# The second batch's q by a casting DMA, and loads in another order, in a fused attention and SwiGLU kernel

## The chip, the cores and the metric

The kernel runs on one core of a Trainium2 chip. The metric is the device time of one execution in microseconds. The kernel before took 332.03 us (median of 3 runs, 331.59 to 332.16). TensorE is the matrix engine (PE in the profile, its weight loads PEld), VectorE is DVE, ScalarE is ACT, GpSimd is POOL, and SyncE (SP) only issues transfers.

## The reference

There are 8 batches of 8 heads with 576 positions and a head width of 64. A linear attention without softmax is normalized per head, its rows become 4608 tokens of width 512, and these go through an RMS norm and a SwiGLU block of inner width 1536:

```python
kv = np.einsum('bhsd,bhse->bhde', k, v)
out = np.einsum('bhsd,bhde->bhse', q, kv)
rms = np.sqrt(np.mean(out * out, axis=-1, keepdims=True) + 1e-06)
x = (out / rms * g_norm)                      # per head, then heads side by side: [4608, 512]
rms = np.sqrt(np.mean(x * x, axis=-1, keepdims=True) + 1e-06)
xn = x / rms * rms_g
g = xn @ w_gate
out = (g * (1.0 / (1.0 + np.exp(-g))) * (xn @ w_val)) @ w_out
```

Inputs and output are float32; the kernel computes its matrix products in bf16 with float32 sums.

## The kernel before

**Tiles.** A batch's 576 positions are four chunks of 128 and a remainder of 64. The remainders of the 8 batches are collected in `xr`, 512 tokens that form a ninth group at the end. So there are nine groups of 512 tokens, each with the same SwiGLU work: for each of 12 column blocks of 128 a gate product (`mm1` with `wg`, L618), its Silu on ScalarE (L627), a value product (`mm1` with `wv`), and the product of the two on VectorE (`h`, L636); then `mm2` (L653) with `wo`, whose results are copied out (L669) and stored by SP (L671). `mm1` rotates over three PSUM buffers: a gate's buffer is freed by its Silu, a value's by its `h`.

**Attention of a batch** goes on beside the SwiGLU of the batch before. q is loaded and made bf16, and is needed transposed (`qTs`). `kv_mm` (L267) forms k'v head by head, with results 64 wide in alternating halves of the partitions; `kv_half` copies the two halves (L291) to `kvs`. `o_mm` (L318) multiplies. The squares of the result are reduced per head, a chain of small VectorE steps turns them into one factor `al` per token and head that holds both norms, and `xna_` (L465) applies it; a transpose then gives `x`.

- The first batch (L774 to L873) is done by hand with transposes on TensorE, spread through the first half of its own SwiGLU. That group is split into two halves of 256 tokens: 22 "early" slots for the first, 12 "half" slots (a gate and a value each) for the second, then 16 "all" slots that run `mm2` block by block (`slots_b_by_j`), three matmuls in each.
- The second batch is placed by hand in `place_second(P, 9)`: numbers are slots relative to the tenth half slot. Its q comes by SP in float32 (`load_q(1)`, released by the last gate weights), is cast by VectorE and ScalarE (L202), and transposed on TensorE by pairs of heads (L297, 128 x 128 each). Its statistics come from a matmul with `sel` (L390) and its factor from the 12-step chain with a bit-trick root (`chain`). The first batch's first half uses a shorter form, `lead_chain` with Sqrt on ScalarE, which needs a `guard` matmul that adds the epsilon (L373).
- Batches 3 to 8 come from `place_attention`, where a `Placer` puts each operation into the first slot with room on its engine. q is loaded by SP in float32 (L180), cast by ScalarE (third batch) or GpSimd (the others), and transposed by a DMA on SP (L311, L313). VectorE reduces the squares (L401), GpSimd weighs them with the gain first (L396).

**Loads.** v, k (from the second batch on) and all weights come by casting DMAs on GpSimd's queue (`load_cast`, `load_w`, `load_wo`), issued in the order of the code: weights, v and k of the second batch, the four pieces of `wo`, k and v of the third batch. There are eight semaphores for these transfers, so each issue waits until the transfer eight places ahead of it has landed. Engines run their instructions in order, so an instruction that waits holds all behind it. Within a slot the operations of other engines are emitted ahead of the slot's own matmuls, those of TensorE behind them. The place of later loads is set at the end of the code (L909 to L920): `P.put` from a given slot on.

Of the kernel before, what the change touches and what calls it, by code (L numbers as in the profile page):

```python
# [86 lines left out]
def kernel(  # L87
# [53 lines left out]
    vc, kc = ([consts.tile([128, H, (NC + 1) * D], BF16, name=f"{t}c{n}") for n in range(2)] for t in "vk")  # L141
    sel = consts.tile([128, 2, 2], BF16, name="sel")
    diag = consts.tile([128, 2 * D], BF16, name="diag")
    ones = consts.tile([1, 128], FP32, name="ones")
    epsr = consts.tile([1, 2 * H], FP32, name="epsr")
    gain = consts.tile([128, NS], FP32, name="gain")
# [37 lines left out]
    def load_cast(b, t, heads=None):  # L184
        to = (vc if t == 2 else kc)[b % 2]
        if heads is None:
            return nc.gpsimd.dma_start(  # L187
                out=to[:REM, :, NC * D :], in_=src[t][b, :, MAIN:S, :].rearrange("h p d -> p h d")
            )
        view = src[t][b, :, 0:MAIN, :].rearrange("h (p c) d -> p h (c d)", c=NC)[:, heads[0] : heads[1]]  # L190
        return nc.gpsimd.dma_start(out=to[:, heads[0] : heads[1], : NC * D], in_=view)  # L191
# [44 lines left out]
    class Att:  # L236
# [56 lines left out]
        def qT_mm(self, js, chunks, pool=None):  # L293
# [7 lines left out]
            return qT_ps  # L301

        def qT_out(self, ps, js, c0, eng):
            copy = eng.copy if eng is nc.scalar else eng.tensor_copy
            n = ps.shape[2] // 128
            to = self.qTj[:, js[0] : js[-1] + 1, c0 : c0 + n, :]
            copy(out=to, in_=ps.rearrange("p j (c t) -> p j c t", t=128))
# [77 lines left out]

        def stat_mm(self, c0, c1):
            self.st = st = att_p.tile([128, 2, NC + 1, H], FP32, name="att")
            for c in range(c0, c1):
                for j in range(NS):
                    nc.tensor.matmul(  # L390
                        st[:, :, c, 2 * j : 2 * j + 2], lhsT=self.sqT[:, j, c], rhs=sel,
                        start=c == c0 and j == 0, stop=c == c1 - 1 and j == NS - 1, skip_group_check=True,
                    )
# [130 lines left out]
    def place_casts(P, b, at=0):  # L524
# [5 lines left out]
        ops = [P.put("POOL", 1.1, lambda hs=hs: cast_main(b, 0, nc.gpsimd, hs), at=at) for hs in (H0, H1)]  # L530
        return [P.put("POOL", 0.65, lambda: cast_rem(b, 0, nc.gpsimd), at=max(at + 9, ops[1][1]))]

# [27 lines left out]
    def place_second(P, s):  # L560
# [7 lines left out]

        dve(-1, 0.7, lambda: cast_main(1, 0, V, H0))
        act(-1, 1.04, lambda: cast_main(1, 0, A, H1))  # L570
        for j in range(NS):
            pe(j // 2, 0.23, ("q", j), lambda j=j: a.qT_mm((j,), range(NC)))
        P.at("PE", 1.14, lambda: a.kv_mm(range(NS)), s)
        dve(1, 0.42, lambda: a.qT_out(ps["q", 0], (0,), 0, V))
        act(1, 0.58, lambda: a.qT_out(ps["q", 1], (1,), 0, A))
        dve(1, 0.43, lambda: a.kv_half(0))
        dve(2, 0.43, lambda: a.kv_half(1))
        dve(2, 0.42, lambda: a.qT_out(ps["q", 2], (2,), 0, V))
        act(2, 0.58, lambda: a.qT_out(ps["q", 3], (3,), 0, A))
        act(2, 0.62, lambda: cast_rem(1, 0, A))  # L580
        pe(3, 0.23, ("q", NC), lambda: a.qT_mm(ALL, (NC,)))
        act(4, 0.58, lambda: a.qT_out(ps["q", NC], ALL, NC, A))

# [5 lines left out]
        for n in range(NC + 1):  # L589
            act((4, 5, 5, 6, 7)[n], 0.62, lambda n=n: a.sqT_(ps["oT", n], *parts[n]))  # L590
            dve((4, 5, 6, 6, 7)[n], 0.69, lambda n=n: a.outa_(n, V))
        P.at("PE", 0.64, lambda: a.stat_mm(0, NC + 1), s + 8)
        dve(9, 2.8, lambda: [f() for f in a.chain(0, NC + 1)])
        for c in range(NC + 1):
# [169 lines left out]
    G.memset(kvs[1], 0.0)  # L764
    for tile_ in (kc[0], kc[1], vc[1]):
        G.memset(tile_[REM:, :, NC * D :], 0.0)
# [44 lines left out]

    for j, pool_, eng in zip(ALL, (o2_p, o2_p, None, mm1_p), (A, A, V, V)):
        a.xT_mm((j,), (0, 1), pool_)
        a.xT_out(j, (0, 1), eng)
# [3 lines left out]
    cast_rem(0, 0, G)  # L818
    for t in (2, 1):
        load_cast(1, t, (0, H))  # L820
        load_cast(1, t)
# [13 lines left out]
    def behind(n):  # L835
# [27 lines left out]
        elif n == 18:  # L863
            a.xna_pairs(held[2], ALL, NC, NC + 1)
        if n in (15, 18):
            i = (15, 18).index(n)
            a.xT_mm((P0, P1)[i], (2, 3), None if i else o2_p)
# [7 lines left out]
    for n, s in enumerate(early):  # L875
        if n == 12:
            gate = load_q(1)
            tc.add_manual_dep(gate.ins, w_loads[-1][0].ins.name, SYNC, reason="the weights come first")
            nc.sync.dma_start(out=gbc, in_=g_norm.partition_broadcast(128))
        emit([s])  # L880
# [5 lines left out]
    gate = load_q(2)  # L886
    tc.add_manual_dep(gate.ins, wo_loads[1].ins.name, SYNC, reason="the weights come first")

# [10 lines left out]
    for b in range(1, B):  # L899
# [16 lines left out]
        elif b + 1 < B:  # L916
            P.put("SP", 0.0, lambda b=b: load_q(b + 1), at=starts[b - 1] + 6 * (b == 2))
            for f in loads_kv(b + 1):
                P.put("POOL", 0.85, f, at=starts[b - 1] + 6)
            casts = place_casts(P, b + 1, starts[b - 1] + 5 + 6 * (b == 2))  # L920
    emit(slots)
# [28 lines left out]
```

## Time and profile before

| | |
|---|---|
| median of 3 runs | 332.03 us |
| profiled execution | 331.74 us |
| its span in the trace | 330.0 us |
| TensorE busy | 318.1 us, 96% of the span |
| VectorE, ScalarE, GpSimd busy | 177.6, 143.1, 86.8 us |
| granted TensorE clock | 1.0 throughout |
| DMA | 41.08 MB, mean 124 GB/s |

Times in the profile are microseconds from the start of the span. A row of the timeline gives the start, the length, the engine, the line of the kernel, the operation, what it writes and reads, and how many instructions are merged; brackets at the end hold the idle time of that engine ahead of it and what ended it. Matmuls are pipelined, and their ends are modelled: successive rows overlap by the tail of the last matmul.

### The profile page before, as it was taken

What the parts mean: (1) busy time and instruction counts of PE and PEld (TensorE: products, weight loads), DVE (VectorE), ACT (ScalarE), POOL (GpSimd) and SP (SyncE); (2) the same over time, 40 slices, a digit from 0 to 9 for tenths busy, and PEclk for the clock granted to TensorE, in tenths of its full rate; (3) what the DMA queues carried; (4) which work ended last, traced back from release to release, by engine and by line L of the source; (5) the groups of instructions that cost most, each with busy time, mean ns of one, the idle gap of its engine ahead of it and who ended that gap; (6) DMA issues with size and microseconds to landing.
All of it is one profiled execution on the core that took longest, in us unless ns stands there. A gap on an engine that the chain in (4) does not pass through costs nothing.

```text
span 330.0 us, 5391 instructions
## 1 busy us (share of the span) xinstructions
PE 318.1 (96%) x2038; PEld 162.6 (49%) x2038; DVE 177.6 (54%) x400; ACT 143.1 (43%) x268; POOL 86.8 (26%) x106
## 2 busy tenths in 40 slices
PE   7899989989999999999999999999999999999995
PEld 2477865544445444544454445444544444444443
DVE  3448557667938780778167816872587234203411
ACT  1474463666548522742275217522752243223320
POOL 8653150026105700580049004900330000000000
PEclk9999999999999999999999999999999999999999
DMA  8999999995367966697869665986000600030014
GB/s 196 225 201 198 238 204 237 185 204 115 73 169 186 137 70 165 178 129 87 170 175 128 89 169 175 114 102 167 35 1 0 167 34 0 2 120 7 0 34 95
DMA packets 78741, 41.08 MB, mean 124 GB/s; under 512 B 42744, under 2 KB 74236, under 8 KB 78716
## 3 DMA queue, kind: packets, MB, share of 16 engines
q1 hardware_dynamic: 47616, 26.25, 34.9%
q0 software_dynamic: 29360, 13.57, 32.4%
q10 hardware_dynamic: 1740, 0.92, 1.0%
q8 instruction: 16, 0.26, 0.3%
q14 instruction: 9, 0.07, 0.1%
HBM read 37.78 MB, written 9.44 MB: 143 GB/s over the span
## 4 chain that ended last, share of the span: by engine, by line
PE 81%; DMA 15%; issue 1%; POOL 1%; DVE 0%; ACT 0%; SPq 0%; POOLq 0%; ACTq 0%
PE mm L618 47%; PE o L653 26%; DMA stg<-in_q_dram 7%; DMA wg<-in_moe_w_gate_dram 6%; DMA vc<-in_v_dram 3%; PE att L318 2%; PE att L267 2%; PE mm L653 2%; PE o L682 1%; POOL sq L396 0%; PE att L297 0%; PE att L355 0%; PE att L491 0%; ACT silu L627 0%; POOL vc L187 0%
## 5 line engine op out<-in xcount | busy, mean ns | idle before, releaser
L636 DVE TENSOR_TENSOR h<-silu,mm 128x512 bf16<-128x512 bf16 (+1 forms) x120 | 75.7, 631 | 80.6 <-PE mm L618 68.2
L627 ACT ACTIVATE silu<-mm 128x512 bf16<-128x512 f32 (+1 forms) x120 | 66.1, 555 | 89.2 <-PE mm L618 81.9
L618 PE MATMUL mm<-x,wv 128*128 128x512 bf16 (+1 forms) x432 | 99.8, 356 | 1.0 <-ACT silu L627 0.9
L618 PE MATMUL mm<-x,wg 128*128 128x512 bf16 (+1 forms) x420 | 98.5, 358 | 1.1 <-DVE h L636 1.1
L653 PE MATMUL o<-wo,h 128*128 128x512 bf16 x396 | 89.9, 379 | 0.0
L396 POOL TENSOR_TENSOR sq<-sq,g 128x512 bf16<-128x512 bf16 x30 | 34.4, 1154 | 131.1 <-ACT sq L344 131.0
L618 PEld LDWEIGHTS <-wg 128*128 128x128 bf16 x468 | 45.2, 98 | 46.8 <-issue 1.4
L618 PEld LDWEIGHTS <-wv 128*128 128x128 bf16 x480 | 45.3, 98 | 42.5 <-issue 1.1
L653 PEld LDWEIGHTS <-h 128*128 128x128 bf16 x420 | 40.4, 98 | 46.8
L669 ACT COPY osb<-o 128x512 f32<-128x512 f32 x33 | 19.3, 588 | 67.9 <-PE o L653 65.9
L401 DVE TENSOR_REDUCE st<-sq 128x8 f32<-128x512 bf16 x60 | 38.5, 679 | 2.1 <-POOL sq L396 2.1
L291 DVE CAST kvs<-att 64x256 bf16<-64x256 f32 x14 | 5.9, 422 | 39.4 <-PE att L267 39.2
L465 DVE TENSOR_TENSOR xna<-outa,al 128x512 bf16<-128x512 bf16 x35 | 21.8, 685 | 0.0
L344 ACT ACTIVATE sq<-att 128x512 bf16<-128x512 f32 x30 | 18.1, 603 | 0.8 <-PE att L318 0.8
L348 ACT CAST outa<-att 128x512 bf16<-128x512 f32 x30 | 17.7, 590 | 0.0
L318 PE MATMUL att<-kvs,qTs 128*128 128x128 bf16 x140 | 11.7, 219 | 1.5 <-DMA qTs<-main_q 1.5
L318 PEld LDWEIGHTS <-qTs 128*128 128x128 bf16 x140 | 9.7, 98 | 7.0 <-DMA qTs<-main_q 2.0
L618 PE MATMUL mm<-xr,wg 128*128 128x512 bf16 x48 | 12.3, 379 | 0.0
L618 PE MATMUL mm<-xr,wv 128*128 128x512 bf16 x48 | 12.3, 379 | 0.0
L202 POOL CAST main_q<-stg 128x1024 bf16<-128x1024 f32 (+1 forms) x12 | 11.4, 978 | 2.9 <-DMA stg<-in_q_dram 2.9
L231 PE MATMUL mm<-idle 128*128 128x512 bf16 x27 | 8.7, 484 | 2.1 <-DVE idle L160 2.1
L191 POOL DMA_DIRECT2D vc<-in_v_dram x9 | 7.9, 877 | 5.4 <-DMA kc<-in_k_dram 4.4
(118 smaller groups left out, 173.9 us busy)
## 6 DMA issues: line engine op xcount, KB each, us to landing
out_dram<-osb SPq DMA_DIRECT2D x32, 256.0 KB, 2.6
stg<-in_q_dram SPq DMA_DIRECT2D x7, 1024.0 KB, 6.9
vc<-in_v_dram POOLq DMA_DIRECT2D x7, 512.0 KB, 7.5
kc<-in_k_dram POOLq DMA_DIRECT2D x7, 512.0 KB, 6.1
wg<-in_moe_w_gate_dram POOLq DMA_DIRECT2D x4, 384.0 KB, 16.2
wv<-in_moe_w_val_dram POOLq DMA_DIRECT2D x4, 384.0 KB, 17.9
wo<-in_moe_w_out_dram POOLq DMA_DIRECT2D x4, 384.0 KB, 18.1
stg<-in_k_dram SPq DMA_DIRECT2D x2, 512.0 KB, 6.6
```

Source lines behind the costliest of these rows:

```text
L202: return copy(out=mains[b, t][:, cs[0] : cs[1], h0:h1, :], in_=staged[b, t].rearrange("p h (c d) -> p c h d", c=NC)[:, cs[0] : cs[1], h0:h ...
L318: nc.tensor.matmul(o[:, 2 * j : 2 * j + 2, :], lhsT=self.qTj[:, j, c, :], rhs=self.kv[:, j, :, :], start=j == 0, stop=j == NS - 1, skip_gr ...
L344: nc.scalar.activation(out=self.sq[c][:, 0], in_=self.o[c], func=ACT.Square)
L348: (eng.tensor_copy if eng else nc.scalar.copy)(out=self.outa[c], in_=self.o[c])
L396: eng.tensor_tensor(out=self.sq[c][:, 1], in0=self.sq[c][:, 0], in1=g2, op=OP.mult)
L401: nc.vector.reduce_sum(out=self.st[:, which, c, :], in_=self.sq[c][:, which], axis=AX.X)
L465: return eng.tensor_tensor(out=self.xna[:, c], in0=src, in1=self.al[:, c, :].to_broadcast([128, H, D]), op=OP.mult)
L618: nc.tensor.matmul(ps[:, : c1 - c0], lhsT=w[n][:, s, jj * 128 : (jj + 1) * 128], rhs=x_of(g, s, c0, c1), start=s == 0, stop=s == NS - 1)
L627: nc.scalar.activation(out=sis[g, j][:, c0:c1], in_=ps, func=ACT.Silu)
L636: nc.vector.tensor_tensor(out=hs[g, j][:, c0:c1], in0=sis[g, j][:, c0:c1], in1=v_ps, op=OP.mult)
L653: nc.tensor.matmul(ps, lhsT=hs[g, j][:, t * 128 : (t + 1) * 128], rhs=wo[j // OB][:, j % OB, :], start=j == 0, stop=j == NF - 1)
L669: (eng.copy if eng is nc.scalar else eng.tensor_copy)(out=o, in_=ps)
```

## The change

The change has these parts.

- The second batch's q comes by a casting DMA on GpSimd's queue into `qc`, ahead of v and k of that batch; `load_q(1)` and its three casts are gone. One more memset on GpSimd clears the remainder's rows of `qc`.
- It is transposed by heads (`qT_heads`): 40 matmuls with results 64 wide in alternating halves of the partitions, in five blocks of 8, in half slots 5 to 9 (counted from one), where 20 matmuls stood in slots 10, 11 and the first "all" slot. `kv_mm` moves from the tenth to the twelfth half slot, both its copies to the slot after it.
- The second batch's factor comes from `lead_chain` (four VectorE steps, Sqrt on ScalarE, one more step), with a guard matmul of 40 columns and two table loads on ScalarE, Sqrt ahead and Silu behind.
- The load of the third batch's q is released by the first piece of `wo` instead of the second.
- The fourth batch's k and v are placed from slot 14 of the second group's SwiGLU on instead of 6, and its q's casts from 18 instead of 11; for the later batches 14 instead of 6 and 18 instead of 5, and the remainder's cast directly behind the others. In GpSimd's program the casts of a batch's q now stand behind all five L396 of the batch before; of the fourth batch's k and v the main piece of k stands ahead of the fifth L396, the rest behind the casts.
- In the first batch, two of the transposes' copies swap between ScalarE and VectorE, and one transpose goes one slot later.

```diff
+    qc = consts.tile([128, H, (NC + 1) * D], BF16, name="qc1")
-    epsr = consts.tile([1, 2 * H], FP32, name="epsr")
+    epsr = consts.tile([1, (NC + 1) * H], FP32, name="epsr")
...
     def load_cast(b, t, heads=None):
-        to = (vc if t == 2 else kc)[b % 2]
+        to = qc if t == 0 else (vc if t == 2 else kc)[b % 2]
...
+        def qT_heads(self, js, chunks):
+            qT_ps = att_p.tile([128, len(js), len(chunks) * 128], BF16, name="att")
+            for n, j in enumerate(js):
+                for i, c in enumerate(chunks):
+                    for half in range(2):
+                        nc.tensor.matmul(
+                            qT_ps[half * D : (half + 1) * D, n, i * 128 : (i + 1) * 128],
+                            lhsT=qc[:, 2 * j + half, c * D : (c + 1) * D], rhs=ident, is_transpose=True,
+                            start=True, stop=True, skip_group_check=True,
+                        )
+            return qT_ps
...
-        def stat_mm(self, c0, c1):
+        def stat_mm(self, c0, c1, guard=False):
             self.st = st = att_p.tile([128, 2, NC + 1, H], FP32, name="att")
+            if guard:
+                nc.tensor.matmul(
+                    st[:, 0, c0:c1, :], lhsT=ones, rhs=epsr[:, : (c1 - c0) * H], start=True, stop=True, skip_group_check=True,
+                )
...
-        return [P.put("POOL", 0.65, lambda: cast_rem(b, 0, nc.gpsimd), at=max(at + 9, ops[1][1]))]
+        return [P.put("POOL", 0.65, lambda: cast_rem(b, 0, nc.gpsimd), at=ops[1][1])]
...
-        dve(-1, 0.7, lambda: cast_main(1, 0, V, H0))
-        act(-1, 1.04, lambda: cast_main(1, 0, A, H1))
         for j in range(NS):
-            pe(j // 2, 0.23, ("q", j), lambda j=j: a.qT_mm((j,), range(NC)))
-        P.at("PE", 1.14, lambda: a.kv_mm(range(NS)), s)
-        dve(1, 0.42, lambda: a.qT_out(ps["q", 0], (0,), 0, V))
-        act(1, 0.58, lambda: a.qT_out(ps["q", 1], (1,), 0, A))
-        dve(1, 0.43, lambda: a.kv_half(0))
-        dve(2, 0.43, lambda: a.kv_half(1))
-        dve(2, 0.42, lambda: a.qT_out(ps["q", 2], (2,), 0, V))
-        act(2, 0.58, lambda: a.qT_out(ps["q", 3], (3,), 0, A))
-        act(2, 0.62, lambda: cast_rem(1, 0, A))
-        pe(3, 0.23, ("q", NC), lambda: a.qT_mm(ALL, (NC,)))
-        act(4, 0.58, lambda: a.qT_out(ps["q", NC], ALL, NC, A))
+            pe(j - 5, 0.25, ("q", j), lambda j=j: a.qT_heads((j,), range(NC)))
+            if j % 2:
+                act(j - 4, 0.58, lambda j=j: a.qT_out(ps["q", j], (j,), 0, A))
+            else:
+                dve(j - 4, 0.42, lambda j=j: a.qT_out(ps["q", j], (j,), 0, V))
+        pe(-1, 0.25, ("q", NC), lambda: a.qT_heads(ALL, (NC,)))
+        act(0, 0.58, lambda: a.qT_out(ps["q", NC], ALL, NC, A))
+        P.at("PE", 1.14, lambda: a.kv_mm(range(NS)), s + 2)
+        dve(3, 0.43, lambda: a.kv_half(0))
+        dve(3, 0.43, lambda: a.kv_half(1))
...
-        P.at("PE", 0.64, lambda: a.stat_mm(0, NC + 1), s + 8)
-        dve(9, 2.8, lambda: [f() for f in a.chain(0, NC + 1)])
+        P.at("PE", 0.64, lambda: a.stat_mm(0, NC + 1, True), s + 8)
+        act(8, 1.28, lambda: A.preload_act_table(ACT.Sqrt))
+        dve(9, 2.0, lambda: a.lead_chain(0, NC + 1))
...
-    for tile_ in (kc[0], kc[1], vc[1]):
+    for tile_ in (kc[0], kc[1], vc[1], qc):
...
-    for j, pool_, eng in zip(ALL, (o2_p, o2_p, None, mm1_p), (A, A, V, V)):
+    for j, pool_, eng in zip(ALL, (o2_p, o2_p, None, mm1_p), (A, V, A, V)):
...
-    for t in (2, 1):
+    for t in (0, 2, 1):
         load_cast(1, t, (0, H))
         load_cast(1, t)
...
-        if n in (15, 18):
-            i = (15, 18).index(n)
+        if n in (16, 18):
+            i = (16, 18).index(n)
...
-            gate = load_q(1)
+            gate = nc.sync.dma_start(out=gbc, in_=g_norm.partition_broadcast(128))
             tc.add_manual_dep(gate.ins, w_loads[-1][0].ins.name, SYNC, reason="the weights come first")
-            nc.sync.dma_start(out=gbc, in_=g_norm.partition_broadcast(128))
...
     gate = load_q(2)
-    tc.add_manual_dep(gate.ins, wo_loads[1].ins.name, SYNC, reason="the weights come first")
+    tc.add_manual_dep(gate.ins, wo_loads[0].ins.name, SYNC, reason="the weights come first")
...
             P.put("SP", 0.0, lambda b=b: load_q(b + 1), at=starts[b - 1] + 6 * (b == 2))
+            casts = place_casts(P, b + 1, starts[b - 1] + 18)
             for f in loads_kv(b + 1):
-                P.put("POOL", 0.85, f, at=starts[b - 1] + 6)
-            casts = place_casts(P, b + 1, starts[b - 1] + 5 + 6 * (b == 2))
+                P.put("POOL", 0.85, f, at=starts[b - 1] + 14)
```

More of the change, by code (lines that the diff above doesn't have):

```diff
@@ L391, in stat_mm @@
                         st[:, :, c, 2 * j : 2 * j + 2], lhsT=self.sqT[:, j, c], rhs=sel,
-                        start=c == c0 and j == 0, stop=c == c1 - 1 and j == NS - 1, skip_group_check=True,
+                        start=not guard and c == c0 and j == 0, stop=c == c1 - 1 and j == NS - 1,
+                        skip_group_check=True,
                     )
```

## The prediction

> **What bounds the kernel now.** I read the page's busy times and its slices first, then TensorE's timeline.
>
> ```profile
> span 330.0 us, 5391 instructions
> ...
> PE 318.1 (96%) x2038; PEld 162.6 (49%) x2038; DVE 177.6 (54%) x400; ACT 143.1 (43%) x268; POOL 86.8 (26%) x106
> ...
> PE   7899989989999999999999999999999999999995
> ```
> TensorE is the bound at 96%, so time can come only out of its own work or its holes. The slices (8.25 us each) show holes early and none later. In the timeline (start, length, engine, line; in brackets the idle time and what ended it) a row's length contains the tail of its last matmul, so I count from start to start.
>
> ```profile
> 40.58 0.60 PE L618 MATMUL mm<-x,wg 128*128 128x256 bf16 x4
> 42.11 0.60 PE L618 MATMUL mm<-x,wv 128*128 128x256 bf16 x4 [0.93 <-ACT silu L627]
> 42.55 0.61 PE L297 MATMUL att<-ident,main_q 128*128 128x128 bf16 x8
> 43.09 0.88 PE L267 MATMUL att<-vc,kc 128*64 128x64 bf16 x40
> 43.90 0.61 PE L618 MATMUL mm<-x,wg 128*128 128x256 bf16 x4
> ...
> 64.47 1.04 PE L618 MATMUL mm<-x,wg 128*128 128x512 bf16 x4
> 65.44 0.56 PE L267 MATMUL att<-vc,kc 128*64 128x64 bf16 x20
> 65.93 1.04 PE L618 MATMUL mm<-x,wv 128*128 128x512 bf16 x4
> 66.80 1.03 PE L618 MATMUL mm<-x,wg 128*128 128x512 bf16 x4
> 69.36 0.62 PE L318 MATMUL att<-kvs,qTs 128*128 128x128 bf16 x8 [1.53 <-DMA qTs<-main_q]
> ...
> 80.85 1.03 PE L618 MATMUL mm<-x,wv 128*128 128x512 bf16 x4
> 82.95 1.02 PE L618 MATMUL mm<-x,wg 128*128 128x512 bf16 x4 [1.07 <-DVE h L636]
> ```
> Four 256-wide matmuls take 0.44 (42.11 to 42.55), four 512-wide ones 0.87 (65.93 to 66.80). So the holes are 42.11 - 40.58 - 0.44 = **1.09**, 69.36 - 66.80 - 0.87 = **1.69** and 82.95 - 80.85 - 0.87 = **1.23** us, together 4.01. Past the third TensorE waits for nothing until the end, so whatever is gained or lost up to there arrives at the end in full.
>
> Who ends these waits, engine by engine, the last row being issue to landing in us:
>
> ```profile
> 40.73 1.04 ACT L202 CAST main_q<-stg 128x1024 bf16<-128x1024 f32 x1 [0.88 <-DMA stg<-in_q_dram]
> ...
> 55.99 1.99 ACT L202 CAST main_q<-stg 128x1024 bf16<-128x1024 f32 x2 [4.26 <-DMA stg<-in_q_dram]
> ```
> ```profile
> 46.00 0.37 SPq L180 DMA_DIRECT2D stg<-in_q_dram  x1
> ...
> 58.00 5.04 SPq L311 DMA_TRANSPOSE qTs<-main_q  x1
> ```
> ```profile
> 78.84 1.04 POOL L202 CAST main_q<-stg 128x1024 bf16<-128x1024 f32 x1 [2.55 <-DMA stg<-in_q_dram]
> ...
> 83.02 0.61 POOL L209 CAST remq<-rstg 64x512 bf16<-64x512 f32 x1
> ```
> ```profile
> qTs<-main_q SPq DMA_TRANSPOSE x1, 11.3
> ```
> Hole 1: ScalarE's cast of the second batch's q waits for its load, and the silu that frees TensorE's PSUM is queued behind it. Hole 2: the third batch's q, loaded from 46.00, lands at 55.99, is cast, and its DMA transpose, issued at 58.00, takes 11.3. Hole 3: GpSimd's cast of the fourth batch's q waits for its load until 78.84; behind it on GpSimd stand squares (L396), behind these reductions on VectorE, and behind these the h that frees PSUM.
>
> **The change part by part.**
>
> *Second batch's q by casting DMA: -1.09.* The casts leave ScalarE and VectorE. What could be late next is the load itself, now on GpSimd's queue in the place where v stood, with v, k and W_out one place later.
>
> ```profile
> 25.77 0.74 POOL L226 DMA_DIRECT2D wo<-in_moe_w_out_dram  x1 [1.17 <-DMA wg<-in_moe_w_gate_dram]
> ...
> 34.72 0.90 POOL L191 DMA_DIRECT2D kc<-in_k_dram  x1 [2.44 <-DMA vc<-in_v_dram]
> ...
> 42.09 0.88 POOL L191 DMA_DIRECT2D vc<-in_v_dram  x1 [4.43 <-DMA kc<-in_k_dram]
> ...
> 48.04 0.88 POOL L191 DMA_DIRECT2D vc<-in_v_dram  x1 [0.95 <-DMA wo<-in_moe_w_out_dram]
> ```
> ```profile
> wo<-in_moe_w_out_dram POOLq DMA_DIRECT2D x4, 384.0 KB, 18.1
> ```
> v had landed by 34.72 and k by 42.09 (GpSimd waited for them), W_out's first piece at 25.77 + 18.1 = 43.9, while q came through SP beside them. The new transposes begin behind the fifth half slot: the tenth begins at 40.58, a slot is 0.87, so 40.58 - 4 x 0.87 = 37.1, over 2 us of cover for a load that takes v's place. kv_mm moves to about 40.58 + 3 x 0.87 + 1.7 for the transposes now ahead of it = 44.9, W_out's first matmul to 45.7. The same bytes are read, so 42.1 and 43.9 should hold as the latest times (two more issues on GpSimd, 0.9 each like the rows, fit into waits like the 2.44). Where that cover is gone, each us late costs one.
>
> *Transposes by heads: +0.6.* The old 20 cost 0.45 per 8 (42.55 to 43.00), 56 ns each, 1.12 in all. The new 40 move 128 columns each, into alternating halves of the partitions, in five blocks. The trace has no such matmul. The nearest rows are kv_mm's, also 64 wide: 20 in 0.49, 40 in 0.81, so 20 to 24.5 ns for 64 columns, which doubled makes 1.6 to 1.96, +0.5 to +0.84. Bounds: halves side by side for the price of the old, 0; one after the other, +1.12, with a gap ahead of each block as ahead of kv_mm (65.44 - 64.47 - 0.87 = 0.10), +1.6. Nothing below nought, since no fewer columns move. I take 0.6, the low end of the doubled rows, because halves alternate here at each matmul and there at each fifth.
>
> The Trainium skill, "TensorEngine Tiling (Array Packing)", Key Properties, says that a change of tiling mode drains TensorE and that tiles of one mode run in parallel; the 0.10 and the 20 ns agree. By its Gotcha 2, column tiling goes without fast weight load; no wait for weights shows in kv_mm's rows, and a price of it here is the second rival.
>
> *kv_mm moved to the slot before W_out: +0.4.* Its two copies (L291) had two slots of cover; now only three matmuls of 0.22, 0.65, stand between kv_mm and oT_mm, which needs both.
>
> ```profile
> 53.12 0.20 DVE L437 TENSOR_SCALAR u<-att 128x40 f32<-128x40 f32 x1 [1.08 <-PE att L390]
> ...
> 56.12 3.10 DVE L465 TENSOR_TENSOR xna<-outa,al 128x512 bf16<-128x512 bf16 x5
> ...
> 66.04 0.86 DVE L291 CAST kvs<-att 64x256 bf16<-64x256 f32 x2 [1.20 <-PE att L267]
> ```
> From kv_mm's end of issue, 65.93, to both copies done, 66.90, is 0.97; with the handover back about 1.05, less 0.65 gives 0.4. Ends: 0 and 1.05.
>
> *Sqrt instead of the 12-step chain: +0.2.* The old chain takes 3.0 (53.12 to 56.12); its product is not waited for by TensorE, so a shorter one gains 0. The guard matmul is added to TensorE:
>
> ```profile
> 13.82 0.39 PE L373 MATMUL mm<-epsr,ones 1*128 1x16 f32 x2
> ```
> I take 0.2 for 40 columns (0.1 to 0.4). ScalarE gets two table loads and a Sqrt.
>
> ```profile
> 16.02 1.28 ACT L423 ACT_TABLE_LOAD   x1
> 17.31 0.84 ACT L501 ACTIVATE x<-o,gain 128x256 bf16<-128x256 bf16 x2
> ```
> The first load hides in the 4.26 that ScalarE idles ahead of 55.99. The chain begins at 53.12 - 1.09 + 0.6 + 0.4 + 0.2 = 53.2; four steps of twelve, 1.4 with the reciprocal, a Sqrt of 0.3 and the load of 1.28 bring it to 56.2. Only then comes the cast of the third batch's q, so it ends near 58.1.
>
> *Third batch's q behind W_out's first piece, with the fourth batch's loads out of its way: -1.69.* Its load may start at 43.9 or earlier and, if it takes the 10 us of 46.00 to 55.99 again, is there by 54; the table load sets the cast. The transpose then starts at 58.1, no earlier than before. TensorE wants it at 67.67 - 1.09 + 1.2 = 67.8, so 9.7 us are to be had where it took 11.3. Beside it ran k and v of the fourth batch: v, issued at 48.04, took 20.8 us, to 68.8. These come now behind the third batch's squares. The fourth batch's transpose, without such loads, took 4.4:
>
> ```profile
> vc<-in_v_dram POOLq DMA_DIRECT2D x1, 512.0 KB, 20.8
> ```
> ```profile
> qTs<-main_q SPq DMA_TRANSPOSE x1, 4.4
> ```
> So I expect it by 62 to 65, and the hole closes. Ends: -1.69 and 0.
>
> *Fourth batch's casts later: -1.23.* They stand behind all five squares, so no square waits for q. The fifth square has one k issue (0.9) ahead of it; two reductions of VectorE and an h cover it, and without them it costs 0.9. Later batches showed no hole, and keep over 10 us between load and use.
>
> *The rest: 0.* A transpose one slot later and a swap of ScalarE and VectorE fill lead-in holes, behind which weights are late anyway:
>
> ```profile
> 31.28 0.77 PEld L618 LDWEIGHTS <-wv 128*128 128x128 bf16 x8 [0.28 <-DMA wv<-in_moe_w_val_dram]
> ```
> TensorE can't pass 31.28 before W_val's last piece (at best -0.3, if that lands earlier without q beside it).
>
> Sum: -4.01 + 0.6 + 0.4 + 0.2 = **-2.8 us**. The profiled execution took 331.74 (its span and 1.74 around it), which gives 328.9. It lies 0.3 below the median of 332.03; on the median, **329.2**.
>
> **The rivals.**
>
> 1. *The third batch's transpose stays late.* It starts as late as before; if it takes 11.3 again, hole 2 stays: 329.2 + 1.7 = 330.9. For it: the second table load on ScalarE. Against it: the 4.4. The Trainium skill, "ScalarE: Activation LUTs", What ACT_TABLE_LOAD costs, puts about 1380 ns of drain beside the load's 1283, which would make the transpose 1.4 later, 59.5; here the next instruction starts at 17.31, 1.29 after the load's start.
>
> 2. *The halves don't run side by side*: +1.6 instead of +0.6, 330.2. For it: no row shows such transposes. Against it: kv_mm's 20 ns.
>
> 3. *The fourth batch's k and v come too late: slower.* v is now issued behind q's casts, which ended at 83.6; less holes 1 and 2 and the added 1.2, 82, and 1.6 for issues ahead, 83.6.
>
> ```profile
> 96.27 0.49 PE att L267 x20
> ```
> ```profile
> vc<-in_v_dram POOLq DMA_DIRECT2D x1, 512.0 KB, 17.5
> ```
> kv_mm wants them at 96.27 - 2.8 = 93.5, so 10 us of landing cost nothing, over 13 turn the gain into a loss; at 17.5, a row with a full queue, the wait is 7.6: 329.2 + 7.6 = 336.8. Against it: by then stores, one q and transposes are all that moves.
>
> 4. *The holes only move*: the two DMAs ahead of k and W_out make these late by about 2.8, 332.0. Against it: cover of 2 or more at each.
>
> **How the numbers follow.** Forecast 0.70, rival 1 0.08, rival 2 0.09, rival 3 0.06, rival 4 0.07. The unknown costs around the forecast reach from 329.2 - 0.6 - 0.4 = 328.2 to 329.2 + 0.65 + 0.2 = 330.1; rivals 1 and 2 carry the range to 331.0: **328.2 to 331.0**, with rivals 3 and 4 and some 0.05 of tails left out. A measurement tells 0.2% (0.66 us) from no change: faster by more are the forecast and rivals 1 and 2, less a little, 0.84; within it most of rival 4 and that little, 0.08; slower 0.08.
>
> **What would show it.** Right: no wait of TensorE for silu near 41, qTs near 68 or h near 82; five blocks of 8 transposes at 0.25 to 0.4 each; one new wait of oT_mm for kvs of 0.2 to 0.5; the third batch's transpose under 8 us. Wrong: kv_mm, o_mm or W_out's first matmul waiting for a DMA, or reductions still waiting for squares.

## The result, and the profile after

The kernel after takes **329.44 us** (median of 4 runs, 329.3 to 329.5), the one before on the same chip 331.81 (4 runs, 331.57 to 332.16): ratio 0.9927, interval 0.991 to 0.9944. 2.4 us are gone, where 2.8 were forecast. The profiled execution took 329.4 us. The added lines move line numbers: `mm1` is now L634, `mm2` L669, `h` L652, `kv_mm` L268, `o_mm` L331, the casts of q L203.

The page of the kernel after, its span, busy times and TensorE's slices:

```profile
span 327.6 us, 5425 instructions
...
PE 318.6 (97%) x2060; PEld 162.2 (49%) x2060; DVE 176.0 (54%) x392; ACT 144.5 (44%) x269; POOL 89.0 (27%) x109
...
PE   7789999999999999999999999999999999999995
```

TensorE is busy 0.5 us longer in a span 2.4 shorter, and no slice from the fourth to the last but one is below 9. Its waits in the kernel after (engine, what, line, whom it waited for; sum, times, longest):

```profile
PE mm L232 <- DVE idle L161: 2.1, 1, 2.1
PE mm L279 <- DMA vc<-in_v_dram: 1.6, 1, 1.6
PE o L509 <- DVE xna L350: 0.5, 1, 0.5
PE att L368 <- DVE kvs L292: 0.3, 1, 0.3
...
```

The first three stand in the lead-in, and those left out are of 0.2. None is for silu, qTs or h: all three holes are closed, and the wait for `kvs` is new. TensorE's timeline after, first around the second batch, then at the places of holes 2 and 3:

```profile
31.07 1.04 PE L634 MATMUL mm<-x,wv 128*128 128x256 bf16 x8
...
36.43 0.60 PE L634 MATMUL mm<-x,wv 128*128 128x256 bf16 x4
36.96 0.41 PE L309 MATMUL att<-ident,qc 128*64 128x128 bf16 x8
37.31 0.61 PE L634 MATMUL mm<-x,wg 128*128 128x256 bf16 x4
...
46.13 0.60 PE L669 MATMUL o<-wo,h 128*128 128x512 bf16 x2
46.58 0.38 PE L669 MATMUL mm<-wo,h 128*128 128x512 bf16 x1
47.23 0.39 PE L368 MATMUL att<-qTs,kvs 128*128 128x512 bf16 x1 [0.28 <-DVE kvs L292]
...
52.25 0.59 PE L669 MATMUL o<-wo,h 128*128 128x512 bf16 x2
52.78 0.41 PE L402 MATMUL att<-epsr,ones 1*128 1x40 f32 x2
53.12 0.65 PE L407 MATMUL att<-sel,sqT 128*128 128x4 bf16 x20
...
67.50 1.03 PE L634 MATMUL mm<-x,wg 128*128 128x512 bf16 x4
68.36 0.61 PE L331 MATMUL att<-kvs,qTs 128*128 128x128 bf16 x8
...
81.56 1.03 PE L634 MATMUL mm<-x,wv 128*128 128x512 bf16 x4
82.43 1.03 PE L634 MATMUL mm<-x,wg 128*128 128x512 bf16 x4
...
84.15 9.88 PE L669 MATMUL o<-wo,h 128*128 128x512 bf16 x45
```

The rows at 67.50 and 81.56 are followed 0.86 and 0.87 later by the next, so `o_mm` and `mm1` start with no idle time ahead. The last row is the first `mm2` of the second group. The same row of the kernel before, and the one that answers to 31.07:

```profile
31.28 1.05 PE L618 MATMUL mm<-x,wv 128*128 128x256 bf16 x8
...
86.40 3.83 PE L653 MATMUL o<-wo,h 128*128 128x512 bf16 x17
```

Between these two marks the change takes effect, but for the swap in the lead-in and the loads of the batches behind the fourth. The first mark hangs on W_val's last piece in most of the kernels and moves between 30.6 and 31.9 in the executions below (32.88 in kernel 8); so I compare kernels by the **stretch** from the eight `wv` matmuls near 31 to the `mm2` near 84. Before it is 86.40 - 31.28 = 55.12 us, after 84.15 - 31.07 = 53.08: 2.04 less.

The other engines after. ScalarE's casts of the third batch's q, with the Sqrt ahead of them:

```profile
54.95 0.24 ACT L440 ACTIVATE nt<-z 128x40 f32<-128x40 f32 x1 [1.68 <-DVE z L437]
55.21 1.28 ACT L441 ACT_TABLE_LOAD   x1
56.50 2.00 ACT L203 CAST main_q<-stg 128x1024 bf16<-128x1024 f32 x2
```

GpSimd: its wait for the second batch's q, and the end of the second group:

```profile
34.00 1.52 POOL L227 DMA_DIRECT2D wo<-in_moe_w_out_dram  x2 [2.22 <-DMA qc<-in_q_dram]
...
79.18 2.02 POOL L203 CAST main_q<-stg 128x1024 bf16<-128x1024 f32 x2
...
82.44 0.89 POOL L192 DMA_DIRECT2D vc<-in_v_dram  x1
```

The second batch's q had landed by 34.00, and the cast of the third's, at 56.50, waits for no DMA. The third batch's transpose is issued at 58.52, not earlier than before (58.00), and is there by 68.36; the profile of this kernel doesn't show when it landed.

### The profile page after: what moved, and what is told of

The parts are those of the page before. It is cut to its first block, busy times and chain, and to the rows that moved or that the text cites. A ratio compares the mean times of both kernels' runs of the same rounds, so it can differ in the third digit from the quotient of the medians.

```text
span 327.6 us, 5425 instructions
## 1 busy us (share of the span) xinstructions
PE 318.6 (97%) x2060; PEld 162.2 (49%) x2060; DVE 176.0 (54%) x392; ACT 144.5 (44%) x269; POOL 89.0 (27%) x109
## 3 DMA queue, kind: packets, MB, share of 16 engines
q1 hardware_dynamic: 46048, 25.08, 31.9%
HBM read 37.78 MB, written 9.44 MB: 144 GB/s over the span
## 4 chain that ended last, share of the span: by engine, by line
PE 94%; DMA 3%; DVE 1%; issue 0%; POOL 0%; ACT 0%; DVEq 0%; POOLq 0%
PE mm L634 57%; PE o L669 26%; DMA vc<-in_v_dram 3%; PE att L331 2%; PE att L268 2%; PE mm L669 2%; PE o L698 1%; PE att L309 1%; PE o L368 0%; DVE xna L350 0%; PE att L509 0%; PE mm L279 0%; PE att L368 0%; PE mm L662 0%; PE mm L232 0%
## 5 line engine op out<-in xcount | busy, mean ns | idle before, releaser
L652 DVE TENSOR_TENSOR h<-silu,mm 128x512 bf16<-128x512 bf16 (+1 forms) x120 | 75.7, 632 | 79.6 <-PE mm L634 69.3
L634 PE MATMUL mm<-x,wv 128*128 128x512 bf16 (+1 forms) x432 | 99.8, 355 | 0.0
L634 PE MATMUL mm<-x,wg 128*128 128x512 bf16 (+1 forms) x420 | 98.7, 358 | 0.0
L669 PE MATMUL o<-wo,h 128*128 128x512 bf16 x396 | 89.9, 379 | 0.0
L634 PEld LDWEIGHTS <-wg 128*128 128x128 bf16 x468 | 45.0, 98 | 45.9
L634 PEld LDWEIGHTS <-wv 128*128 128x128 bf16 x480 | 45.4, 98 | 40.9
L669 PEld LDWEIGHTS <-h 128*128 128x128 bf16 x420 | 40.3, 98 | 46.9
L331 PEld LDWEIGHTS <-qTs 128*128 128x128 bf16 x140 | 9.8, 98 | 5.2
L634 PE MATMUL mm<-xr,wg 128*128 128x512 bf16 x48 | 12.3, 379 | 0.0
L634 PE MATMUL mm<-xr,wv 128*128 128x512 bf16 x48 | 12.3, 379 | 0.0
L331 PE MATMUL att<-kvs,qTs 128*128 128x128 bf16 x140 | 11.7, 219 | 0.0
L203 POOL CAST main_q<-stg 128x1024 bf16<-128x1024 f32 (+1 forms) x12 | 11.4, 987 | 0.1
L232 PE MATMUL mm<-idle 128*128 128x512 bf16 x27 | 8.0, 455 | 2.1 <-DVE idle L161 2.1
L786 ACT ACTIVATE wv<-wv,gain 128x384 bf16<-128x384 bf16 x16 | 9.2, 612 | 0.2 <-PE mm L634 0.2
```

Of the source, the lines that this page charges most:

```text
L203: return copy(out=mains[b, t][:, cs[0] : cs[1], h0:h1, :], in_=staged[b, t].rearrange("p h (c d) -> p c h d", c=NC)[:, cs[0] : cs[1], h0:h ...
L331: nc.tensor.matmul(o[:, 2 * j : 2 * j + 2, :], lhsT=self.qTj[:, j, c, :], rhs=self.kv[:, j, :, :], start=j == 0, stop=j == NS - 1, skip_gr ...
L634: nc.tensor.matmul(ps[:, : c1 - c0], lhsT=w[n][:, s, jj * 128 : (jj + 1) * 128], rhs=x_of(g, s, c0, c1), start=s == 0, stop=s == NS - 1)
L652: nc.vector.tensor_tensor(out=hs[g, j][:, c0:c1], in0=sis[g, j][:, c0:c1], in1=v_ps, op=OP.mult)
L669: nc.tensor.matmul(ps, lhsT=hs[g, j][:, t * 128 : (t + 1) * 128], rhs=wo[j // OB][:, j % OB, :], start=j == 0, stop=j == NF - 1)
```

## The experiments

The prediction says that hole 2 closes because k and v of the fourth batch no longer run beside the transpose, and hole 3 because that batch's casts stand behind the squares. The rival, which the prediction doesn't have and which came up after runs 1 to 4: neither order is needed, and the second batch's q in bf16 closes them. Then come the three prices. Ratios are to the kernel before, run beside each; its medians were 331.99, 332.31 and 331.92.

| kernel | median us (range) | ratio (interval) | stretch us |
|---|---|---|---|
| after | 329.44 (329.3 to 329.5) | 0.9927 (0.991 to 0.9944) | 53.08 |
| 1 old release of third q | 329.56 (329.15 to 329.7) | 0.9925 (0.9906 to 0.9943) | 53.08 |
| 2 k, v early | 329.30 (329.11 to 329.45) | 0.9917 (0.9896 to 0.9938) | 53.09 |
| 3 casts early | 329.57 (329.49 to 329.86) | 0.9929 (0.9911 to 0.9947) | 53.20 |
| 4 both early | 329.42 (329.26 to 329.69) | 0.9923 (0.9905 to 0.9941) | 53.35 |
| 5 third and fourth loads as before | 329.47 (329.38 to 330.23) | 0.9928 (0.9907 to 0.9949) | 53.08 |
| 6 before, later loads alone | 329.70 (328.88 to 329.82) | 0.9923 (0.9898 to 0.9949) | 53.39 |
| 7 old chain | 329.02 (328.73 to 329.69) | 0.9912 (0.9891 to 0.9933) | 52.64 |
| 8 kv_mm a slot earlier | 328.89 (328.75 to 330.76) | 0.9919 (0.9887 to 0.9951) | 52.63 |
| 9 transposes by halves | 329.40 (329.19 to 329.5) | 0.9924 (0.9906 to 0.9943) | 53.12 |
| 10 transposes of pairs | 328.97 (328.83 to 329.61) | 0.9916 (0.9896 to 0.9935) | 51.95 |
| 11 = 7 + 8 | 328.25 (328.03 to 328.92) | 0.9895 (0.9878 to 0.9913) | 52.19 |
| 12 = 7 + 8 + 10 | 327.88 (327.5 to 328.19) | 0.9879 (0.9859 to 0.9898) | 51.05 |

The profiled execution of 8 took 330.76 us, 1.8 above its next run. Its lead-in ends later, with the mark at 32.88, so only its stretch, 85.51 - 32.88, and rows within it are read.

**1. The third batch's q released by the second piece of W_out again**, the rest as after.

```diff
-    tc.add_manual_dep(gate.ins, wo_loads[0].ins.name, SYNC, reason="the weights come first")
+    tc.add_manual_dep(gate.ins, wo_loads[1].ins.name, SYNC, reason="the weights come first")
```

> The changed kernel with one part undone: the third batch's q is again released by the second piece of W_out. It was issued at 42.66 in the changed kernel and will be issued near 44.6; with the 10 us of the kernel before it lands by 54.6, ahead of the end of ScalarE's table load at 56.5, which sets the cast. My theory (hole 2 closed because the fourth batch's k and v no longer run beside the transpose): no change, 329.4, and no wait of o_mm for qTs. Rival (the earlier release closed it): a wait of up to 1.7 us comes back, 331.1.

Measured 329.56, the stretch the same, the transpose issued at 58.86. The earlier release buys nothing.

**2. The fourth batch's k and v early**, the casts behind the squares.

```diff
+            early_kv = b == 2
+            if early_kv:
+                for f in loads_kv(b + 1):
+                    P.put("POOL", 0.85, f, at=starts[b - 1] + 6)
...
-            for f in loads_kv(b + 1):
-                P.put("POOL", 0.85, f, at=starts[b - 1] + 14)
+            if not early_kv:
+                for f in loads_kv(b + 1):
+                    P.put("POOL", 0.85, f, at=starts[b - 1] + 14)
```

> The changed kernel with only the fourth batch's k and v issued early again, behind the third batch's in GpSimd's queue; its q's casts stay behind the five squares. My theory: the transpose of the third batch's q again shares the DMA engines with them and takes 9 to 11 us instead of some 5; it starts at 58.5 and is wanted at 68.4, so o_mm waits 0 to 1.5 us: 329.4 to 330.9, likeliest 330.4. The fourth batch's q lands later too, but no square stands behind its casts. Rival (the earlier release closed hole 2): no wait, 329.4.

Measured 329.30, stretch 53.09, no wait for `qTs`. The transposes now run beside k and v, as before the change, and are still in time. So hole 2 doesn't need the reason that I gave.

**3. The fourth batch's casts between the squares**, k and v late.

```diff
-            casts = place_casts(P, b + 1, starts[b - 1] + 18)
+            casts = place_casts(P, b + 1, starts[b - 1] + (11 if b == 2 else 18))
```

> The changed kernel with only the casts of the fourth batch's q placed from slot 11 again, so that they stand between the third batch's squares; its k and v stay late. The prediction's theory (the casts' place behind the squares closes hole 3): the hole comes back, h waits for squares up to 1.2 us, 330.6. Rival (the load now lands by 72 because k and v are out of its way, so the casts wait for nothing wherever they stand): 329.4 to 329.7, with TensorE waiting 0 to 0.3.

Measured 329.57, stretch 53.20. The first cast starts at 74.22 without waiting for its load: of hole 3 are left 0.12, the 0.12 by which the stretch exceeds that of after. So hole 3 doesn't need the casts' place either.

**4. Both early** (the edits of 2 and 3 together).

> The changed kernel with both undone for the fourth batch: its k and v issued early and its q's casts between the squares, as in the kernel before. Both holes should show again, hole 2 with 0 to 1.5 and hole 3 with about 1.2: 330.6 to 332.1, likeliest 331.6. If the casts' place alone sets hole 3, this run equals the sum of the two runs that undo one each; if the load's landing sets it, hole 3 shows here and in neither of them.

Measured 329.42. GpSimd's timeline, then TensorE's, of this kernel:

```profile
76.66 1.04 POOL L203 CAST main_q<-stg 128x1024 bf16<-128x1024 f32 x1 [1.49 <-DMA stg<-in_q_dram]
```
```profile
79.64 1.03 PE L634 MATMUL mm<-x,wv 128*128 128x512 bf16 x4
80.77 1.02 PE L634 MATMUL mm<-x,wg 128*128 128x512 bf16 x4
```

The cast waits for its load again, with squares behind it, but 2.2 us earlier than before's 78.84. Of hole 3 is left 80.77 - 79.64 - 0.86 = 0.27, the 0.27 by which the stretch exceeds that of after. Hole 2 stays closed.

**5. The third and the fourth batch's loads as before**: edits 1, 2 and 3 together. Ahead of the end of the stretch, only the second batch's part of the change is left (and the lead-in's swap); the batches behind the fourth stay as after.

> The changed kernel with every later load as in the kernel before: the third batch's q released by the second piece of W_out, the fourth batch's k and v early and its q's casts between the squares. Only the second batch's own parts remain. New theory, after the four runs that undid one part or two and lost nothing: the second batch's q as bf16 writes half the bytes, so the whole queue behind it drains some 3 us earlier, and this alone closes holes 2 and 3. It expects no wait for qTs over 0.5 us and none for squares over 0.5: 329.4 to 330.2. Rival (the release of the third batch's q and the fourth batch's order cover for each other, either is enough, but not neither): a wait of 1 us or more for qTs or for squares, 330.6 to 332.3.

Measured 329.47, the stretch 53.08 as after. In SP's timeline of this kernel transposes run as late as before, and beside the same k and v; GpSimd's shows the cast's wait once more:

```profile
58.69 1.41 SPq L324 DMA_TRANSPOSE qTs<-main_q  x1
60.21 4.75 SPq L326 DMA_TRANSPOSE qTs<-remq  x1
```
```profile
48.39 0.89 POOL L192 DMA_DIRECT2D vc<-in_v_dram  x1
...
76.15 1.04 POOL L203 CAST main_q<-stg 128x1024 bf16<-128x1024 f32 x1 [0.61 <-DMA stg<-in_q_dram]
```

TensorE reaches `o_mm` at 68.53 and the place of hole 3 at 80.87 without idle time. So **the second batch's part alone closes all three holes.** What it does to the others is in the DMA engines. The page's line on all DMA, before and then in this kernel:

```profile
DMA packets 78741, 41.08 MB, mean 124 GB/s; under 512 B 42744, under 2 KB 74236, under 8 KB 78716
```
```profile
DMA packets 78741, 40.49 MB, mean 124 GB/s; under 512 B 42744, under 2 KB 74236, under 8 KB 78716
```

A window of before (engines' busy times, at the end the clock, the DMA engines' share and GB/s), and v of the fourth batch from issue to landing in this kernel (for before it is the prediction's row of 20.8):

```profile
58.00:62.00 4.00, 4.00 (x31) 2.10 (x29) 3.54 (x12) 3.59 (x9) 0.00 (x0) 1.00 1.60 189
```
```profile
vc<-in_v_dram POOLq DMA_DIRECT2D x1, 512.0 KB, 16.9
```

Kernels 4 and 5 and the one after move 0.59 MB less: q of the second batch, 576 x 512 values, at 2 bytes less each. In before's windows of 4 us from 38 to 74 the share is always above 1 (1.60 is the highest, 1.07 the last), so the times of the packets overlap and there is work for the engines throughout. If so, bytes saved ahead come back as time. An estimate: at the 161 to 267 GB/s of these windows 0.59 MB are 2.2 to 3.7 us, at the 189 of the row shown 3.1. v landed at 48.04 + 20.8 = 68.8 before and at 48.39 + 16.9 = 65.3 here, in kernel 4 at 48.02 + 17.7 = 65.7: 3.1 to 3.5 earlier. The fourth batch's q lands 2.2 to 2.7 earlier. Hole 2 was 1.69, and `o_mm` itself is wanted 0.9 later (68.53 for 67.67), so 0.8 was enough. That it is the bytes agrees in size at each place, but it isn't shown: the same part of the change also moves q from SP to GpSimd's queue, ahead of v and k, and no run separates the two.

**6. The later loads alone**, on the kernel before: q of the second batch stays float32 through SP, with its old transposes and chain.

```diff
-        return [P.put("POOL", 0.65, lambda: cast_rem(b, 0, nc.gpsimd), at=max(at + 9, ops[1][1]))]
+        return [P.put("POOL", 0.65, lambda: cast_rem(b, 0, nc.gpsimd), at=ops[1][1])]
...
+            casts = place_casts(P, b + 1, starts[b - 1] + 18)
             for f in loads_kv(b + 1):
-                P.put("POOL", 0.85, f, at=starts[b - 1] + 6)
-            casts = place_casts(P, b + 1, starts[b - 1] + 5 + 6 * (b == 2))
+                P.put("POOL", 0.85, f, at=starts[b - 1] + 14)
```

> The kernel before with only the later loads' order changed: k and v from the fourth batch on behind the squares, casts behind all five. The second batch's q still comes by SP in float32. If the fourth batch's k and v beside the transpose were a sufficient cause of holes 2 and 3, both close here and hole 1 stays, without the price of the transposes by heads, the guard and the copies of kv: 332.0 - 1.7 - 1.2 = 329.1. If the float32 q of the second batch is a necessary part of it: hole 2 stays at least in part, 329.6 to 331.

Measured 329.70, inside the second range expected, but not for its reason: holes 2 and 3 are closed here as well. So **either part is enough for them, and their gains don't add**; by the ratio, the later loads alone (0.9923) and the second batch's part alone (0.9928) each gain as much as the whole change (0.9927), within the intervals. With k and v out of its way the third batch's transpose takes 4.3 instead of 11.3, as the prediction has it:

```profile
qTs<-main_q SPq DMA_TRANSPOSE x1, 4.3
```

What closes hole 3 here, the casts' place or a load of q with k and v out of its way, this run doesn't separate. Two other waits stand in their place. TensorE's timeline of this kernel, and ScalarE's:

```profile
42.28 0.82 PE L267 MATMUL att<-vc,kc 128*64 128x64 bf16 x36 [0.18 <-DMA kc<-in_k_dram]
...
58.35 0.39 PE L491 MATMUL att<-ident,xna 128*128 128x128 bf16 x4
60.28 0.38 PE L491 MATMUL att<-ident,xna 128*128 128x128 bf16 x4 [1.54 <-ACT x L501]
```
```profile
56.14 1.99 ACT L202 CAST main_q<-stg 128x1024 bf16<-128x1024 f32 x2 [5.28 <-DMA stg<-in_q_dram]
...
58.88 0.62 ACT L209 CAST remq<-rstg 64x512 bf16<-64x512 f32 x1 [0.76 <-DMA rstg<-in_q_dram]
```

`kv_mm` waits for k of the second batch and takes 1.25 from start to start (41.78 to 43.03), where it took 0.81 before. The remainder of the third batch's q lands at 58.88; ScalarE waits for it, and behind its cast stands the copy that TensorE needs; from start to start that hole is 60.28 - 58.35 - 0.22 = 1.71. Hole 1 is 0.17 in this execution, since the second batch's q had landed by 39.43. Why that q came earlier than before's 40.73, and the remainder later than before, the edit doesn't say.

**7. The 12-step chain back**, without guard matmul and table loads.

```diff
-        P.at("PE", 0.64, lambda: a.stat_mm(0, NC + 1, True), s + 8)
-        act(8, 1.28, lambda: A.preload_act_table(ACT.Sqrt))
-        dve(9, 2.0, lambda: a.lead_chain(0, NC + 1))
+        P.at("PE", 0.64, lambda: a.stat_mm(0, NC + 1), s + 8)
+        dve(9, 2.8, lambda: [f() for f in a.chain(0, NC + 1)])
```

> The changed kernel with the second batch's factor by the 12-step chain again: no guard matmul, no Sqrt, no table loads. Theory: the guard costs TensorE 0.44 us (52.68 to 53.12 in its timeline) and buys nothing, since the transposes behind it never waited for the chain: 329.4 - 0.4 = 329.0. The cast of the third batch's q would then start as soon as that q has landed, showing when that is. Rival (the longer chain is late now): a wait of the first transpose for xna, 0.1 to 1 us, and 329.4 or more.

Measured 329.02, the stretch 0.44 shorter. Its TensorE timeline:

```profile
53.04 0.59 PE L668 MATMUL o<-wo,h 128*128 128x512 bf16 x2
53.47 0.64 PE L407 MATMUL att<-sel,sqT 128*128 128x4 bf16 x20
```

`sel` follows 0.43 after the two `wo`; with the guard it was 53.12 - 52.25 = 0.87. The difference, 0.44, is the guard.

**8. kv_mm one slot earlier**, so that its copies have a whole slot of cover.

```diff
-        P.at("PE", 1.14, lambda: a.kv_mm(range(NS)), s + 2)
-        dve(3, 0.43, lambda: a.kv_half(0))
-        dve(3, 0.43, lambda: a.kv_half(1))
+        P.at("PE", 1.14, lambda: a.kv_mm(range(NS)), s + 1)
+        dve(2, 0.43, lambda: a.kv_half(0))
+        dve(2, 0.43, lambda: a.kv_half(1))
```

> The changed kernel with kv_mm of the second batch one half slot earlier and its two copies in the next: the wait of oT_mm for kvs, 0.43 us from start to start, goes, 329.0. Its inputs are there: k's remainder landed at 27.2 + 13.6 = 40.8 and kv_mm would start near 44. Rival (the wait only moves, to a copy of q's last transposes or to PSUM): 329.4.

Measured 328.89. Its TensorE timeline:

```profile
47.96 0.38 PE L669 MATMUL o<-wo,h 128*128 128x512 bf16 x1
48.39 0.38 PE L669 MATMUL mm<-wo,h 128*128 128x512 bf16 x1
48.60 0.38 PE L368 MATMUL att<-qTs,kvs 128*128 128x512 bf16 x1
```

0.64 from the first `wo` to `oT_mm`, where it was 47.23 - 46.13 = 1.10: the wait for `kvs` is gone, and the stretch is 0.45 shorter. By the time alone the gain is within the spread of the runs.

**9. The transposes by halves**: four into one half of the partitions, then four into the other, instead of alternating.

```diff
-                for i, c in enumerate(chunks):
-                    for half in range(2):
+                for half in range(2):
+                    for i, c in enumerate(chunks):
```

> The changed kernel with the transposes by heads in another order only: in each block the four of one half of the partitions, then the four of the other, instead of alternating. Theory (neighbours on different halves run partly side by side, which is why a block of 8 takes 0.35 us or 43 ns each and not 0.45): blocks of 0.42 to 0.45 now, five times +0.07 to +0.1, 329.8 to 329.9. Rival (a 64-wide transpose simply costs 43 ns, whatever its neighbour): blocks stay at 0.35, 329.4.

Measured 329.40. A block of 8 and the matmuls behind it, TensorE's timeline:

```profile
37.08 0.42 PE L309 MATMUL att<-ident,qc 128*64 128x128 bf16 x8
37.43 0.61 PE L634 MATMUL mm<-x,wg 128*128 128x256 bf16 x4
```

0.35 for 8, as in the alternating order (36.96 to 37.31). The neighbour's half makes no difference.

**10. Transposes of pairs of heads, 20 of them**: q comes by four casting DMAs, chunk by chunk, so that two heads lie side by side in `qc`.

```diff
-    qc = consts.tile([128, H, (NC + 1) * D], BF16, name="qc1")
+    qc = consts.tile([128, NC + 1, H, D], BF16, name="qc1")
...
+            for c in range(NC):
+                last = nc.gpsimd.dma_start(
+                    out=qc[:, c], in_=src[0][b, :, 0:MAIN, :].rearrange("h (p c) d -> c p h d", c=NC)[c]
+                )
...
-                            qT_ps[half * D : (half + 1) * D, n, i * 128 : (i + 1) * 128],
-                            lhsT=qc[:, 2 * j + half, c * D : (c + 1) * D], rhs=ident, is_transpose=True,
+                        qT_ps[:, n, i * 128 : (i + 1) * 128],
+                        lhsT=qc[:, c, 2 * j : 2 * j + 2, :], rhs=ident, is_transpose=True,
```

> The changed kernel with the second batch's q still by casting DMA, but laid out by chunks in four DMAs, so that two heads are one operand of 128 columns and 20 transposes do. Theory (the transposes by heads cost 1.13 us more than the old ones): TensorE gets 1.1 back, 328.3. Rival (the load now writes runs of 128 bytes instead of 512 and takes longer; v, k and W_out wait behind it): the first transpose, kv_mm or W_out's first matmul waits for its DMA, each us late costs one, 328.3 to 331; W_out's first piece had 3 us of cover.

Measured 328.97, half the gain expected. Its TensorE timeline:

```profile
36.55 0.60 PE L644 MATMUL mm<-x,wv 128*128 128x256 bf16 x4
36.98 0.39 PE L319 MATMUL att<-ident,qc 128*128 128x128 bf16 x4
37.21 0.60 PE L644 MATMUL mm<-x,wg 128*128 128x256 bf16 x4
...
94.72 1.02 PE L644 MATMUL mm<-x,wg 128*128 128x512 bf16 x4 [0.47 <-DMA x<-xna]
```

A block costs 0.23 with no gap ahead (36.55 + 0.44 = 36.99), and the stretch is 1.13 shorter, as expected. Behind the stretch, in this execution, a DMA transpose of the third batch's `xna` comes 0.47 late and takes part of it back. Kernel 12 has no such wait, so it doesn't go with the edit; why it came here stays open.

**11. Edits 7 and 8 together, and 12, edits 7, 8 and 10 together.**

> The changed kernel with the 12-step chain instead of Sqrt and with kv_mm one half slot earlier, both in one. If the two prices (0.44 guard, 0.43 wait for kvs) are TensorE's own, they add up: 329.4 - 0.9 = 328.5. Rival (the cast of the third batch's q or the chain ends late once TensorE is earlier): a wait for xna or qTs shows, 328.8 to 329.4.

> The same with 20 transposes by pairs as well. If all three prices add up: 329.4 - 1.1 - 0.4 - 0.4 = 327.4. If the slower load of q delays k, which kv_mm now wants some 2 us earlier than in the changed kernel: a wait of kv_mm for k of 0.5 to 2 us, 328 to 329.5.

Measured 328.25 and 327.88. By the stretches the prices add: 53.08 - 52.19 = 0.89 for 0.44 + 0.46, and 53.08 - 51.05 = 2.03 for these and 1.13. TensorE's marks in kernel 12:

```profile
31.36 1.05 PE L643 MATMUL mm<-x,wv 128*128 128x256 bf16 x8
...
82.41 7.93 PE L678 MATMUL o<-wo,h 128*128 128x512 bf16 x36
```

Kernel 12 is the fastest, 4.0 us below before. Of the stretch's 2.03 the profiled executions show 329.40 - 327.66 = 1.74, as the first mark comes 0.29 later here than in the kernel after; the medians show 1.6.

## Why the prediction came out right, step by step

The time and the holes are as forecast, but **two of the three holes close without the reason given**, and two prices were too low. The costs are 2.00 where 1.2 were forecast, 0.8 more, and yet the time is only 0.24 above the forecast. That is luck: the mark near 31 came 0.21 earlier, the kernel before measured 0.22 lower this time (331.81 for 332.03), and some 0.1 lies behind the second mark.

- *Hole 1, -1.09: right.* q had landed by 34.00, and its transposes begin at 36.96.
- *Transposes by heads, +0.6: too low, +1.13.* From the `wv` row at 36.43 to the `wg` row at 37.31 are 0.88, of which the four `wv` matmuls take 0.44; so 0.44 or 0.45 a block, 2.25 for five, less the old 1.12. The transposes alone are 40 x 43 ns = 1.72, 0.6 above the old, and that was the value taken. What failed is that the gap of 0.10 ahead of each block, quoted for `kv_mm`, entered only the upper bound. By the Trainium skill, "TensorEngine Tiling (Array Packing)", Key Properties, every change of tiling mode drains TensorE; the trace agrees, with 0.09 to 0.10 ahead of each block of 64-wide matmuls and none ahead of kernel 10's 128-wide ones. Rival 2 named 1.6 as well, for halves that don't run side by side. Kernel 9 shows 43 ns a transpose in either order, so the alternating halves, the prediction's reason for its low end, don't matter; whether the halves overlap at all stays open, as 43 is less than the 56 of a 128-wide one. The price lies about halfway between 0.6 and 1.6.
- *kv_mm moved, +0.4: right*, 47.23 - 46.58 - 0.22 = 0.43.
- *Guard, +0.2: too low, +0.44* (kernel 7), just above the bound of 0.4: the gap again, 52.78 - 52.25 - 0.43 = 0.10, and 0.34 for the two float32 rows.
- *Sqrt and table loads, 0: right.* The cast of the third batch's q begins at 56.50, 0.01 after the load's end, and ends near 58.5, forecast 58.1. By the Trainium skill, "ScalarE: Activation LUTs", What ACT_TABLE_LOAD costs, about 1380 ns of drain would come besides; these rows show none.
- *Third batch's q and the fourth's k and v, -1.69: the hole closes, the reason isn't needed.* With k and v beside the transpose again (kernels 2, 4, 5) and the old release (1, 5) it stays closed. That reason alone would have been enough: in kernel 6 the transpose takes 4.3, near the 4.4 that the prediction quotes. Rival 1 counted on it too. What the prediction left out is the second batch's part: it reckoned that the same bytes are read (37.78 MB on both pages, which is right) and put nothing on the 0.59 MB less that are moved. With that part alone v lands 3.5 earlier and the hole closes (kernel 5).
- *Fourth batch's casts later, -1.23: the hole closes, the reason is only one of two.* The casts between the squares cost 0.12 (kernel 3), 0.27 (kernel 4) or nothing (kernel 5), since their load comes over 2 us earlier. The prediction counted on the casts' place alone.
- *The rest, 0:* the mark near 31 moved by -0.21, inside its spread.
- *Rival 3* had the right cover: v of the fourth batch is issued at 82.44 and lands in 8.2, at 90.6, and its remainder, issued at 83.32, in 8.9, at 92.2, against 93.96, where `kv_mm` starts without a wait.
- *Rival 4* didn't come: neither `kv_mm` nor the first matmul of W_out (46.13) waits for a DMA.

The sum with the measured sizes: -4.01 + 1.13 + 0.43 + 0.44 = -2.01, and the stretch shows -2.04. With the -0.21 ahead of it that is 86.40 - 84.15 = 2.25, of the 2.4 by which span and median fell. Of what the holes gave back, half is spent inside the change itself.

## What to carry to other kernels

Where the DMA engines are full up to the place where a transfer is late, look for bytes to save or to move away ahead of it; here either closed the holes, and two edits that close the same hole gain it once. Price a small matmul of another form as its own length plus a gap ahead of every block (0.10 here), and prefer few blocks, or a layout in which the wide form serves. Before a gain is put down to one part of a change, undo that part alone and look whether the wait returns.

## What the runs showed that was not expected

- A transpose with a 64-wide result costs 43 ns (0.35 for 8) in either order of the halves, one 128 wide 56 ns (0.45 for 8): half the width saves a quarter, not half.
- A float32 matmul pair of 40 columns and one row of weights takes 0.34 us and a gap of 0.10, nearly as long as two bf16 matmuls of 512 columns (0.43).
- In eleven of the fourteen kernels TensorE's weight load at the mark near 31 waits for W_val's last piece, and there the mark varies from 30.62 (kernel 11) to 31.85 (kernel 7), so differences of a few tenths between single executions are read inside the stretch.
